# KV products and their fold into the output weights by single heads in small TensorE tiles, and another layout of the modulation weights at the start, in a transformer block on one Trainium2 core

## The chip, the cores and the metric

The kernel runs on one core of one Trainium2 chip. The time is device microseconds (us) of that core; lower is better. Every timed run below is of the fast state; a run taken once has no state, and it is used for its trace. Within the fast state runs still differ in the TensorE clock that was granted to them, by 0.1 to 0.5% of the span; that turns out to matter here. "PE" is TensorE (matmuls), "PEld" its weight loads, "DVE" VectorE, "ACT" ScalarE, "POOL" GpSimd, "SP" the engine that issues most DMA. A line number such as L98 is that of the kernel's source; nearly all matmuls go through one helper (L98), so they are told apart by the tiles that they write and read.

## The reference, cut to what matters

```python
x = A_x                                       # 1 x 2048 x 1024, bf16
mod = (silu(c) @ w_mod).reshape(1, 6, 1, -1)  # w_mod 1024 x 6144
sa, ca, ga, sb, cb, gb = ...                  # the six rows of mod
h = layernorm(x) * (1 + ca) + sa
x = x + ga * A(h)                             # linear attention, 32 heads of width 32
h = layernorm(x) * (1 + cb) + sb
x = x + gb * B(h)                             # SwiGLU, 1024 -> 3584 -> 1024

# A, for each head:
pq, pk = phi(q), phi(k)                       # phi(t) = t+1 if t > 0 else exp(t), + 1e-6
kv = einsum('bhsd,bhse->bhde', pk, v)         # 32 x 32 per head
z  = sum of pk over the sequence              # 32 per head
o  = (pq @ kv) / (pq @ z + 1e-6)
return concat_heads(o) @ wo
```

Two things matter. The matrix `kv` of a head is only 32 x 32, so a 128 x 128 product of four heads computes sixteen blocks and needs four. And nothing can start before `silu(c) @ w_mod` has given `sa` and `ca`.

## The kernel before

The sequence is cut into four parts of 512 rows. Each part gets its k and v; `kv` is summed over the parts; then `kv` is multiplied into `wo` once ("the fold", 16 matmuls), so that attention is one product of `pq` with the folded `wo`. The feed-forward part, some 600 us, follows and is not touched.

The KV products, four heads to a 128-wide matmul, with a 129th column of ones for `z`:

```python
def kv_phase(sc):
    for hg0 in range(0, HG, 3):
        nh = min(3, HG - hg0)
        kvp = acc_b("kvp")                    # acc_b: a PSUM bank, four in rotation
        kvv = kvp[:, 0:3 * (P + 1)].rearrange("p (g e) -> p g e", e=P + 1)
        for i in range(nh):
            for t in range(STC):
                mm(kvv[:, i, :], lhsT=pks[sc][:, t, (hg0 + i) * P:(hg0 + i + 1) * P],
                   rhs=vs[sc][:, t, hg0 + i, 0:P + 1], start=(t == 0), stop=(t == STC - 1))
        ...                                   # DVE adds it to kv_acc
```

The fold, after the 128 x 128 blocks have been masked to their diagonal 32 x 32 blocks (KVZ) and transposed (KVT):

```python
wf = [(hg, nb) for hg in range(HG) for nb in range(NNB)]
for qc in range(5, 11):
    q_phase(1 + qc // 8, qc % 8, qc % 8 + 1)            # 8 matmuls of 216 ns
    for hg, nb in wf[3 * (qc - 5):3 * (qc - 4)]:
        ps = acc_b("wf")
        w = wo[hg // 4][:, hg % 4, nb * NB:(nb + 1) * NB]
        mm(ps[:], lhsT=KVT[:, hg, :], rhs=w, start=True, stop=True)
        nc.scalar.copy(out=w, in_=ps[:])
```

The start. `c` comes as 8 values to a partition, and `w_mod` accordingly 8 consecutive rows to a partition; 20 matmuls on zeros (`keep_warm`) fill the time until the first x has been normalised:

```python
wm_v = w_mod.rearrange("(p j) n -> p j n", j=DC)
c_v = c.rearrange("o (p j) -> p (o j)", j=DC)
...
keep_warm(spare, 20)
with in_order(nc.vector, nc.scalar, nc.gpsimd):         # these engines keep program order
    nc.scalar.activation(out=scT[:], in_=c_sb[:], func=ACT.Silu)
    xns = [ln1_norm(*ln1_stats(0, t)) for t in range(3)]    # the last step is on ACT
    mod_ps = acc_b("mod_ps")
    pe_transpose_tile(hT, xns[0], 0, DC)
    keep_warm(spare, 1)
    mod_block(0, 1, 0, 4)                               # 32 matmuls of one column
    pe_transpose_tile(hT, xns[1], 1, DC)
    ...
    mod_block(0, 0, 0, 2)                               # needs the second w_mod block
    for cc in (0, 1):
        modulate(hT, cc, ca1T, saT, 0, H)
    mod_block(0, 0, 2, 4)
    ...
    k_mms(0, gs, accs, 0, 3)                            # "the first k matmuls"
```

Of the kernel before, what the change touches and what calls it, by code (L numbers as in the profile page):

```python
# [21 lines left out]
def kernel(  # L22
# [13 lines left out]
    nc = tc.nc  # L36
# [16 lines left out]
    FPB = FBW // P  # L53
    VW = P + 2
    GPT = 8
# [5 lines left out]
    wqkv_v = A_wqkv.rearrange("(c p) n -> p c n", p=P)  # L61
    wo_v = A_wo.rearrange("(c p) n -> p c n", p=P)
    wg_v = B_w_gate.rearrange("(c p) f -> p c f", p=P)
    wu_v = B_w_up.rearrange("(c p) f -> p c f", p=P)
    wd_v = B_w_down.rearrange("(f p) n -> p f n", p=P)
    wm_v = w_mod.rearrange("(p j) n -> p j n", j=DC)
    c_v = c.rearrange("o (p j) -> p (o j)", j=DC)

# [34 lines left out]
    def big(name, shape):  # L103
        return k8.tile([P] + shape, BF16, name=name, tag="k8")
# [8 lines left out]

    c_sb = const.tile([P, DC], BF16, name="c_sb")

# [62 lines left out]
    gb_bc = const.tile([P, D], BF16, name="gb_bc")  # L178
    kvs = k8.tile([P, HG * VW + HG * P], F32, name="kvs", tag="k8")
    kv_acc = kvs[:, 0:HG * VW].rearrange("p (g e) -> p g e", e=VW)  # L180
    kvb = kvs[:, HG * VW:].bitcast(BF16).rearrange("p (k g e) -> p k g e", k=2, e=P)
    KVZ, KVT = kvb[:, 0], kvb[:, 1]
    Zden = const.tile([P, HG, DH], BF16, name="Zden")
    kvmask = const.tile([P, P], BF16, name="kvmask")
    zmask = const.tile([P, HG, DH], BF16, name="zmask")
    sel = const.tile([P, HPC, P], BF16, name="sel")

    def build_masks():
        nc.gpsimd.memset(kvmask[:], 0.0)
        nc.gpsimd.memset(zmask[:], 0.0)  # L190
        for h in range(HPC):
            rs = slice(h * DH, (h + 1) * DH)
            nc.gpsimd.memset(kvmask[rs, rs], 1.0)
            for hg in range(HG):
                nc.gpsimd.memset(zmask[rs, hg, HG * h + hg:HG * h + hg + 1], 1.0)
            nc.gpsimd.memset(sel[h * DH:h * DH + 1, h, :], 1.0)
# [103 lines left out]
    def v_phase(sc):  # L300
        v = big("v", [STC, HG, VW])
        vs[sc] = v
        nc.gpsimd.memset(v[:, :, :, P:VW], 1.0)
        for t in range(STC):
            for nb in range(NNB):
                acc = acc_a()
                for cc in range(DC):
                    mm(acc[:], lhsT=hTs[sc][:, cc, t * P:(t + 1) * P],
                                     rhs=wv[cc // 4][:, cc % 4, nb * NB:(nb + 1) * NB],
                                     start=(cc == 0), stop=(cc == DC - 1))  # L310
                nc.scalar.copy(out=v[:, t, nb * 4:(nb + 1) * 4, 0:P], in_=acc[:].rearrange("p (g e) -> p g e", e=P))  # L311

    def q_phase(sc, lo=0, hi=DC):
        if lo == 0:
            pqs[sc] = big("pq", [HG, SCW])
        for qc in range(lo, hi):
# [4 lines left out]
            phi_to(pqs[sc][:, qc, :], acc[:])  # L321

    def kv_phase(sc):
        for hg0 in range(0, HG, 3):
            nh = min(3, HG - hg0)
            kvp = acc_b("kvp")
            kvv = kvp[:, 0:3 * (P + 1)].rearrange("p (g e) -> p g e", e=P + 1)
            for i in range(nh):
                for t in range(STC):
                    mm(kvv[:, i, :], lhsT=pks[sc][:, t, (hg0 + i) * P:(hg0 + i + 1) * P],  # L330
                                     rhs=vs[sc][:, t, hg0 + i, 0:P + 1], start=(t == 0), stop=(t == STC - 1))
            dst = kv_acc[:, hg0:hg0 + nh, 0:P + 1]
            if sc == 0:
                nc.vector.tensor_copy(out=dst, in_=kvv[:, 0:nh, :])
            else:
                nc.vector.tensor_tensor(out=dst, in0=dst, in1=kvv[:, 0:nh, :], op=ALU.add)

# [87 lines left out]
    with in_order(nc.vector, nc.scalar, nc.gpsimd):  # L425
        nc.scalar.activation(out=scT[:], in_=c_sb[:], func=ACT.Silu)
        xns = [ln1_norm(*ln1_stats(0, t)) for t in range(3)]
        mod_ps = acc_b("mod_ps")
        pe_transpose_tile(hT, xns[0], 0, DC)
        keep_warm(spare, 1)  # L430
        mod_block(0, 1, 0, 4)
        pe_transpose_tile(hT, xns[1], 1, DC)
        keep_warm(spare, 1)
        pe_transpose_tile(hT, xns[2], 2, DC // 2)
        keep_warm(spare, 3)
        mod_block(0, 0, 0, 2)
        for cc in (0, 1):
            modulate(hT, cc, ca1T, saT, 0, H)
        mod_block(0, 0, 2, 4)
        for cc in (2, 3):  # L440
            modulate(hT, cc, ca1T, saT, 0, H)
        k_mms(0, gs, accs, 0, 3)
# [6 lines left out]
        gs7, accs7 = k_groups[6:7], [acc_b("acc")]  # L449
        k_mms(0, gs7, accs7, 0, 4)  # L450
        mod_block(1, 0, 0, 2)
        for cc in (4, 5):
            modulate(hT, cc, ca1T, saT)
        k_mms(0, gs + gs7, accs + accs7, 4, 5)
        k_mms(0, gs[0:4], accs[0:4], 5, 6)
# [15 lines left out]
    for sc in range(NSC):  # L471
        if sc > 0:
            k_phase(sc, 0, 2)
            kv_phase(sc - 1)
            if sc >= 2:
                row = mod_rows(blks)
            k_phase(sc, 2, 4)
            if sc == 2:
                mod_bc(row)
            if sc == 3:  # L480
                mod_cols(row)
            k_phase(sc, 4, 8)
            if sc == 1:
                blks = mod_load([2 * D, 2 * D + NB, 5 * D, 5 * D + NB])
            if sc == 2:
                blks = mod_load([3 * D, 3 * D + NB, 4 * D, 4 * D + NB])
# [14 lines left out]
        if sc == 2:  # L501
            wo = load_w(wo_v, 0, "wo")
            for cc in range(DC):
                w = wo[cc // 4][:, cc % 4, :]
                nc.vector.tensor_tensor(out=w, in0=w, in1=ga_bc, op=ALU.mult)

    q_phase(1, 0, 2)
    kv_phase(NSC - 1)
    for h in range(2):
        hs = slice(4 * h, 4 * h + 4)  # L510
        nc.vector.tensor_tensor(out=KVZ[:, hs, :], in0=kv_acc[:, hs, 0:P],
                                in1=kvmask[:].unsqueeze(1).to_broadcast([P, 4, P]), op=ALU.mult)
        nc.vector.tensor_tensor(out=Zden[:, hs, :], in0=kv_acc[:, hs, P:P + 1].to_broadcast([P, 4, DH]),
                                in1=zmask[:, hs, :], op=ALU.mult)
    q_phase(1, 2, 4)
    tpk = acc_b("tp", (HG, P), BF16)
    for hg in range(HG):
        transpose(tpk[:, hg, :], KVZ[:, hg, :])
    nc.scalar.copy(out=KVT[:, 0:4, :], in_=tpk[:, 0:4, :])
    nc.vector.tensor_copy(out=KVT[:, 4:8, :], in_=tpk[:, 4:8, :])  # L520
    den_sum(0)
    den_spread(0)
    q_phase(1, 4, 5)
    wf = [(hg, nb) for hg in range(HG) for nb in range(NNB)]
    for qc in range(5, 11):
        q_phase(1 + qc // 8, qc % 8, qc % 8 + 1)
        for hg, nb in wf[3 * (qc - 5):3 * (qc - 4)]:
            ps = acc_b("wf")
            w = wo[hg // 4][:, hg % 4, nb * NB:(nb + 1) * NB]
            mm(ps[:], lhsT=KVT[:, hg, :], rhs=w, start=True, stop=True)  # L530
            nc.scalar.copy(out=w, in_=ps[:])

# [151 lines left out]
```

## Time and profile before

| | before |
|---|---|
| median of the first 4 runs | 844.27 us (843.91 to 845.21) |
| span of the profiled run | 841.5 us |
| PE busy | 833.8 us, 99% of the span |
| start of one matmul to the next in the stream, 512 / 128 / 129 / 1 columns (N) | 216 / 56 / 57 / 25 ns |
| one phase of KV products, four of them | 1.81 us |
| the fold, 16 matmuls | 3.46 us |

From the page of the kernel before, the busy time of each engine (us, share of the span, number of instructions), and the chain of work that ended last, by engine:

```profile
PE 833.8 (99%) x4289; PEld 385.5 (46%) x4289; DVE 306.8 (36%) x599; ACT 176.2 (21%) x268; POOL 55.6 (7%) x163
...
PE 98%; DMA 1%; SPq 0%; DVE 0%; issue 0%
```

The chain is PE nearly from end to end: what shortens PE's stream shortens the kernel, and what runs beside it does not. The chain in order of time (start, length in us, what) gives the parts that the change touches:

```profile
63.10 1.81 PE kvp L98 x32
...
161.85 0.45 PE tp L101 x8
...
166.42 0.65 PE wf L98 x3
167.06 1.73 PE acc L98 x8
168.79 0.65 PE wf L98 x3
```

A phase of KV products (`kvp`) is 32 matmuls at the 57 ns rate; the fold (`wf`) is five groups of three and one of one, each behind a q block of 1.73 us.

The start of the kernel before, from its timeline (start, length, engine, line, operation, out<-in, and in brackets how long the engine had been idle and what ended that):

```profile
1.21 7.00 PE L98 MATMUL acc<-sel 128*128 128x512 bf16 x20 [1.21 <-DVE sel L412]
...
5.23 0.21 ACT L426 ACTIVATE scT<-c_sb 128x8 bf16<-128x8 bf16 x1 [3.23 <-DMA c_sb<-in_c_dram]
...
10.69 0.95 PE L98 MATMUL mod_ps<-scT,wme 128*128 128x1 bf16 x32 [1.83 <-DMA wme<-in_w_mod_dram]
...
13.55 0.55 PE L98 MATMUL mod_ps<-scT,wme 128*128 128x1 bf16 x16
...
14.78 4.06 PE L98 MATMUL acc<-wk,hT 128*128 128x512 bf16 x18
```

Here Silu (`scT`) runs as soon as `c` has landed, PE waits for both `w_mod` blocks, and the first k matmul begins at 14.78 us.

### The profile page before, as it was taken

Reading aid. Unit: us, or ns where it says so; the run is one execution under the profiler, and the core shown is the slowest. Engines: PE = TensorE matmul, PEld = TensorE weight load, DVE = VectorE, ACT = ScalarE, POOL = GpSimd, SP = SyncE. Lnnn points to the kernel's source line nnn. Section 1 sums busy time; section 2 is a strip of 40 time slices with the busy share of each in tenths; the row PEclk is TensorE's granted clock in tenths of the full one; section 3 lists DMA queues with packets and bytes.
Section 4 is the critical chain, followed back from the end, with each engine's and each line's share of the span. In section 5 each row is a group of like instructions: output and inputs, shape, how many; then the busy total and the mean of one; then the engine's idle time right before and its main releaser. Section 6 shows DMA issues by size and latency. Waiting matters only on the chain.

```text
span 841.5 us, 10528 instructions
## 1 busy us (share of the span) xinstructions
PE 833.8 (99%) x4289; PEld 385.5 (46%) x4289; DVE 306.8 (36%) x599; ACT 176.2 (21%) x268; POOL 55.6 (7%) x163
## 2 busy tenths in 40 slices
PE   8999999999999999999999999999999999999998
PEld 4444444544444444444444444444444444444444
DVE  5656563467523324432221344211124432111122
ACT  3355353354211111101111010111110101111000
POOL 3011010112050001100000010000001100000000
PEclk9999999999999999999999999999999999999999
DMA  9895770029998545528434073581504629720011
GB/s 304 308 248 122 232 188 1 2 52 250 348 236 251 193 145 175 154 70 257 151 100 150 25 233 106 178 260 52 198 1 131 182 69 315 238 66 1 17 60 50
DMA packets 127232, 128.74 MB, mean 153 GB/s; under 512 B 33616, under 2 KB 108880, under 8 KB 126672
## 3 DMA queue, kind: packets, MB, share of 16 engines
q1 hardware_dynamic: 123600, 115.36, 45.7%
q0 software_dynamic: 3584, 12.72, 4.9%
q8 instruction: 33, 0.54, 0.3%
q14 instruction: 15, 0.12, 0.1%
HBM read 108.01 MB, written 12.71 MB: 143 GB/s over the span
## 4 chain that ended last, share of the span: by engine, by line
PE 98%; DMA 1%; SPq 0%; DVE 0%; issue 0%
PE acc L98 89%; PE a_ps L98 7%; DMA wme<-in_w_mod_dram 1%; PE kvp L98 1%; PE modr L98 0%; PE wf L98 0%; PE mod_ps L98 0%; PE den L98 0%; SPq L120 0%; PE tp L101 0%; PE bcr L98 0%; SPq L131 0%; SPq L125 0%; DVE hT L221 0%; PE mcol L98 0%
## 5 line engine op out<-in xcount | busy, mean ns | idle before, releaser
L98 PE MATMUL acc<-h2T,wgu 128*128 128x512 bf16 x1792 | 387.6, 379 | 0.0
L98 PEld LDWEIGHTS <-wgu 128*128 128x128 bf16 x1792 | 175.0, 98 | 211.6
L98 PE MATMUL acc<-wd,gu 128*128 128x512 bf16 (+2 forms) x924 | 196.1, 373 | 0.0
L591 DVE TENSOR_TENSOR gu<-acc,e 128x512 bf16<-128x512 f32 x112 | 77.5, 692 | 299.3 <-PE acc L98 296.5
L590 ACT ACTIVATE e<-acc 128x512 f32<-128x512 f32 x112 | 66.9, 597 | 374.8 <-PE acc L98 374.8
L98 PEld LDWEIGHTS <-gu 128*128 128x128 bf16 x924 | 89.2, 98 | 104.6
L98 PEld LDWEIGHTS <-hT 128*128 128x128 bf16 x512 | 49.4, 98 | 60.3 <-DVE hT L221 1.3
L612 DVE TENSOR_TENSOR e<-acc,gb_bc 128x512 f32<-128x512 f32 (+2 forms) x33 | 22.3, 676 | 131.3 <-PE acc L98 131.3
L98 PE MATMUL acc<-wk,hT 128*128 128x512 bf16 x256 | 57.6, 379 | 0.7 <-DVE hT L221 0.7
L98 PE MATMUL a_ps<-wo,pq 128*128 128x512 bf16 x256 | 57.4, 379 | 0.0
L98 PE MATMUL acc<-hT,wq 128*128 128x512 bf16 x256 | 57.1, 379 | 0.0
L98 PE MATMUL acc<-wv,hT 128*128 128x512 bf16 x256 | 55.9, 379 | 0.0
L273 ACT ACTIVATE eb<-acc 128x512 bf16<-128x512 f32 x64 | 37.9, 596 | 63.4 <-PE acc L98 60.3
L218 ACT ACTIVATE xn<-x,nmr,rstd 128x1024 bf16<-128x1024 f32 x16 | 19.8, 1240 | 126.3 <-POOL nmr L216 126.3
L274 DVE TENSOR_SCALAR eb<-eb 128x512 bf16<-128x512 bf16 x64 | 18.4, 291 | 58.7 <-ACT eb L273 58.6
L98 PEld LDWEIGHTS <-pq 128*128 128x128 bf16 x256 | 25.0, 98 | 30.3
L98 PEld LDWEIGHTS <-wq 128*128 128x128 bf16 x256 | 24.9, 98 | 29.8
L559 POOL DMA_DIRECT2D x_scratch<-x x16 | 9.6, 600 | 418.6 <-DVE x L552 418.6
L552 DVE TENSOR_TENSOR x<-a_ps,x_sb 128x512 f32<-128x512 f32 x32 | 22.1, 692 | 8.2 <-PE a_ps L98 8.1
L202 POOL TENSOR_TENSOR rstd<-veps,neg_half 128x1 f32<-128x1 f32 x32 | 18.0, 562 | 86.0 <-DVE veps L200 75.2
L311 ACT CAST v<-acc 128x512 bf16<-128x512 f32 x32 | 18.3, 582 | 22.0 <-PE acc L98 22.0
L615 DVE TENSOR_TENSOR ob<-e,x1r 128x512 bf16<-128x512 f32 (+2 forms) x33 | 22.3, 675 | 1.0
(72 smaller groups left out, 276.9 us busy)
## 6 DMA issues: line engine op xcount, KB each, us to landing
wgu<-in_B_w_gate_dram SPq DMA_DIRECT2D x28, 1024.0 KB, 7.5
wgu<-in_B_w_up_dram SPq DMA_DIRECT2D x28, 1024.0 KB, 8.7
x_sb<-in_A_x_dram SPq DMA_DIRECT2D x32, 256.0 KB, 6.7
wml<-in_w_mod_dram SPq DMA_DIRECT2D x8, 1024.0 KB, 8.6
x_scratch<-x POOLq DMA_DIRECT2D x16, 512.0 KB, 3.1
x1r<-x_scratch SPq DMA_DIRECT2D x31, 256.0 KB, 2.9
wd<-in_B_w_down_dram SPq DMA_DIRECT2D x7, 1024.0 KB, 5.6
rbc<-rden_scratch POOLq DMA_DIRECT2D x16, 256.0 KB, 5.2
```

What stands on the lines that cost most here:

```text
L98: return tc.keep_in_program_order(nc.tensor.matmul(out, lhsT=lhsT, rhs=rhs, start=start, stop=stop))
L202: nc.gpsimd.tensor_tensor(out=rstd[:, 0:n], in0=veps[:, 0:n], in1=neg_half[:].to_broadcast([P, n]), op=ALU.pow)
L218: nc.scalar.activation(out=dst, in_=src, func=ACT.Identity, bias=nmr[:], scale=rstd[:, 0:1])
L273: nc.scalar.activation(out=e[:], in_=acc, func=ACT.Exp)
L274: nc.vector.tensor_scalar(out=e[:], in0=e[:], scalar1=1.0, scalar2=PHI_EPS, op0=ALU.min, op1=ALU.add)
L311: nc.scalar.copy(out=v[:, t, nb * 4:(nb + 1) * 4, 0:P], in_=acc[:].rearrange("p (g e) -> p g e", e=P))
L552: nc.vector.tensor_tensor(out=x1[:, ns], in0=a_ps[:], in1=x_t[:, ns], op=ALU.add)
L559: nc.gpsimd.dma_start(out=x1_dram[st * P:(st + 1) * P, :], in_=x1[:])
L590: nc.scalar.activation(out=sg[:], in_=ps[0][:], func=ACT.Silu)
L591: gm = nc.vector.tensor_tensor(out=guT[sc][f // GPT][:, f % GPT, :], in0=ps[1][:], in1=sg[:], op=ALU.mult)
L612: nc.vector.tensor_tensor(out=yt, in0=y_ps, in1=gb_bc[:, ns], op=ALU.mult)
L615: nc.vector.tensor_tensor(out=ob, in0=yt, in1=x1r, op=ALU.add)
```

## The change

It does four things. The KV products go head by head: a matmul has 32 weight columns and writes 32 PSUM partitions, so that four heads stand side by side in the array ("column tiles"), and 64 moving columns (32 of v, 32 ones) in place of 129. The fold goes head by head too, in 32 x 32 tiles, 16 at once, which needs `wo` loaded in another order and 2 transposes in place of 8. `w_mod` rows are taken in blocks of 128, so that `c` can be loaded as 8 contiguous rows and turned by a matmul. And the first k matmuls and the modulation rows are re-paced.

The diff, cut to its core (masks, pool shapes and views are left out):

```diff
-    wm_v = w_mod.rearrange("(p j) n -> p j n", j=DC)
-    c_v = c.rearrange("o (p j) -> p (o j)", j=DC)
+    wm_v = w_mod.rearrange("(j p) n -> p j n", p=P)
+    c_v = c.rearrange("o (j p) -> (o j) p", p=P)
...
     def kv_phase(sc):
-        for hg0 in range(0, HG, 3):
-            ... (shown above)
+        kvp = acc_b("kvp", (HG, 2, DH))
+        for hg in range(HG):
+            for t in range(STC):
+                for i in range(HPC):
+                    mm(kvp[i * DH:(i + 1) * DH, hg, :, :],
+                       lhsT=pks[sc][:, t, hg * P + i * DH:hg * P + (i + 1) * DH],
+                       rhs=v_ones(vs[sc], t * D + hg * P + i * DH), start=(t == 0), stop=(t == STC - 1))
...
-        nc.scalar.activation(out=scT[:], in_=c_sb[:], func=ACT.Silu)
+        mod_ps = acc_b("mod_ps")
+        mm(mod_ps[:, 0:DC], lhsT=c_sb[:], rhs=ident[0:DC, 0:DC], start=True, stop=True)
+        nc.scalar.activation(out=scT[:], in_=mod_ps[:, 0:DC], func=ACT.Silu)
         xns = [ln1_norm(*ln1_stats(0, t)) for t in range(3)]
-        mod_ps = acc_b("mod_ps")
         pe_transpose_tile(hT, xns[0], 0, DC)
         keep_warm(spare, 1)
-        mod_block(0, 1, 0, 4)
         pe_transpose_tile(hT, xns[1], 1, DC)
         keep_warm(spare, 1)
+        mod_block(0, 1, 0, 4)
...
-        mod_block(0, 0, 0, 2)
-        for cc in (0, 1):
-            modulate(hT, cc, ca1T, saT, 0, H)
-        mod_block(0, 0, 2, 4)
-        for cc in (2, 3):
-            modulate(hT, cc, ca1T, saT, 0, H)
+        for lo, hi in ((0, 1), (1, 4)):
+            mod_block(0, 0, lo, hi)
+            for cc in range(lo, hi):
+                modulate(hT, cc, ca1T, saT, 0, H)
...
-        k_mms(0, gs7, accs7, 0, 4)
+        k_mms(0, gs7, accs7, 0, 2)
         mod_block(1, 0, 0, 2)
         for cc in (4, 5):
             modulate(hT, cc, ca1T, saT)
+        k_mms(0, gs7, accs7, 2, 4)
...
             kv_phase(sc - 1)
+            k_phase(sc, 2, 4)
             if sc >= 2:
                 row = mod_rows(blks)
-            k_phase(sc, 2, 4)
+            k_phase(sc, 4, 6)
...
-    q_phase(1, 4, 5)
-    (16 matmuls of 128 x 128 x 512, three behind each q block, shown above)
+    def fold_wo(h, nb):
+        ns = slice(nb * NB, (nb + 1) * NB)
+        ps = [acc_b("wf") for _ in range(4)]
+        for i in range(HPC):
+            for g in range(4):
+                rs = slice(g * DH, (g + 1) * DH)
+                mm(ps[g][i * DH:(i + 1) * DH, :], lhsT=KVT[rs, h, i * DH:(i + 1) * DH], rhs=wo[h][rs, i, ns],
+                   start=True, stop=True)
+        for g in range(4):
+            (nc.scalar.copy if g % 2 == 0 else nc.vector.tensor_copy)(out=wo[h][:, g, ns], in_=ps[g][:])
+
+    q_phase(1, 4, 6)
+    fold_wo(0, 0)
+    q_phase(1, 6, 8)
+    fold_wo(0, 1)
+    q_phase(2, 0, 2)
+    fold_wo(1, 0)
+    q_phase(2, 2, 3)
+    fold_wo(1, 1)
```

More of the change, by code (lines that the diff above doesn't have):

```diff
@@ L53 @@
     FPB = FBW // P
-    VW = P + 2
+    VT = STC * D
     GPT = 8
@@ L61 @@
     wqkv_v = A_wqkv.rearrange("(c p) n -> p c n", p=P)
-    wo_v = A_wo.rearrange("(c p) n -> p c n", p=P)
+    wo_v = A_wo.rearrange("(h g i e) n -> h g e i n", h=2, g=4, i=HPC)
     wg_v = B_w_gate.rearrange("(c p) f -> p c f", p=P)
@@ L112 @@
     x1_dram = dram.tile([S, D], F32, name="x1_scratch")
-    c_sb = const.tile([P, DC], BF16, name="c_sb")
+    c_sb = const.tile([DC, P], BF16, name="c_sb")
     x_tiles = {}
@@ L178 @@
     gb_bc = const.tile([P, D], BF16, name="gb_bc")
-    kvs = k8.tile([P, HG * VW + HG * P], F32, name="kvs", tag="k8")
-    kv_acc = kvs[:, 0:HG * VW].rearrange("p (g e) -> p g e", e=VW)
-    kvb = kvs[:, HG * VW:].bitcast(BF16).rearrange("p (k g e) -> p k g e", k=2, e=P)
-    KVZ, KVT = kvb[:, 0], kvb[:, 1]
+    kvs = k8.tile([P, HG * (2 * DH + 1)], F32, name="kvs", tag="k8")
+    kv_acc = kvs[:, 0:HG * (DH + 1)].rearrange("p (g e) -> p g e", e=DH + 1)
+    kvb = kvs[:, HG * (DH + 1):].bitcast(BF16)
+    KVB = kvb[:, 0:HG * DH].rearrange("p (g e) -> p g e", e=DH)
+    KVT = kvb[:, HG * DH:].rearrange("p (h e) -> p h e", e=P)
     Zden = const.tile([P, HG, DH], BF16, name="Zden")
-    kvmask = const.tile([P, P], BF16, name="kvmask")
     zmask = const.tile([P, HG, DH], BF16, name="zmask")
@@ L188, in build_masks @@
     def build_masks():
-        nc.gpsimd.memset(kvmask[:], 0.0)
         nc.gpsimd.memset(zmask[:], 0.0)
@@ L192, in build_masks @@
             rs = slice(h * DH, (h + 1) * DH)
-            nc.gpsimd.memset(kvmask[rs, rs], 1.0)
             for hg in range(HG):
@@ L300, in v_phase @@
     def v_phase(sc):
-        v = big("v", [STC, HG, VW])
+        v = big("v", [VT + DH])
         vs[sc] = v
-        nc.gpsimd.memset(v[:, :, :, P:VW], 1.0)
+        nc.gpsimd.memset(v[:, VT:], 1.0)
         for t in range(STC):
@@ L310, in v_phase @@
                                      start=(cc == 0), stop=(cc == DC - 1))
-                nc.scalar.copy(out=v[:, t, nb * 4:(nb + 1) * 4, 0:P], in_=acc[:].rearrange("p (g e) -> p g e", e=P))
+                nc.scalar.copy(out=v[:, t * D + nb * NB:t * D + (nb + 1) * NB], in_=acc[:])
     def q_phase(sc, lo=0, hi=DC):
@@ L321, in q_phase, with v_ones @@
             phi_to(pqs[sc][:, qc, :], acc[:])
+    def v_ones(v, lo):
+        head = v[:, lo:lo + DH]
+        return bass.AP(head.tensor, head.offset, [list(head.ap[0]), [VT - lo, 2], [1, DH]])
     def kv_phase(sc):
-        for hg0 in range(0, HG, 3):
-            nh = min(3, HG - hg0)
-            kvp = acc_b("kvp")
-            kvv = kvp[:, 0:3 * (P + 1)].rearrange("p (g e) -> p g e", e=P + 1)
-            for i in range(nh):
-                for t in range(STC):
-                    mm(kvv[:, i, :], lhsT=pks[sc][:, t, (hg0 + i) * P:(hg0 + i + 1) * P],
-                                     rhs=vs[sc][:, t, hg0 + i, 0:P + 1], start=(t == 0), stop=(t == STC - 1))
-            dst = kv_acc[:, hg0:hg0 + nh, 0:P + 1]
-            if sc == 0:
-                nc.vector.tensor_copy(out=dst, in_=kvv[:, 0:nh, :])
-            else:
-                nc.vector.tensor_tensor(out=dst, in0=dst, in1=kvv[:, 0:nh, :], op=ALU.add)
+        kvp = acc_b("kvp", (HG, 2, DH))
+        for hg in range(HG):
+            for t in range(STC):
+                for i in range(HPC):
+                    mm(kvp[i * DH:(i + 1) * DH, hg, :, :], lhsT=pks[sc][:, t, hg * P + i * DH:hg * P + (i + 1) * DH],
+                       rhs=v_ones(vs[sc], t * D + hg * P + i * DH), start=(t == 0), stop=(t == STC - 1))
+        kvv = kvp[:].rearrange("p g k e -> p g (k e)")[:, :, 0:DH + 1]
+        if sc == 0:
+            nc.vector.tensor_copy(out=kv_acc, in_=kvv)
+        else:
+            nc.vector.tensor_tensor(out=kv_acc, in0=kv_acc, in1=kvv, op=ALU.add)
     def mod_load(cols):
@@ L481 @@
                 mod_cols(row)
-            k_phase(sc, 4, 8)
+            k_phase(sc, 6, 8)
             if sc == 1:
@@ L501 @@
         if sc == 2:
-            wo = load_w(wo_v, 0, "wo")
+            wo = [big("wo", [4, D]) for _ in range(2)]
+            for h in range(2):
+                for g in range(4):
+                    nc.sync.dma_start(out=wo[h][g * DH:(g + 1) * DH, :, :], in_=wo_v[h, g])
             for cc in range(DC):
@@ L508 @@
     kv_phase(NSC - 1)
-    for h in range(2):
-        hs = slice(4 * h, 4 * h + 4)
-        nc.vector.tensor_tensor(out=KVZ[:, hs, :], in0=kv_acc[:, hs, 0:P],
-                                in1=kvmask[:].unsqueeze(1).to_broadcast([P, 4, P]), op=ALU.mult)
-        nc.vector.tensor_tensor(out=Zden[:, hs, :], in0=kv_acc[:, hs, P:P + 1].to_broadcast([P, 4, DH]),
-                                in1=zmask[:, hs, :], op=ALU.mult)
-    q_phase(1, 2, 4)
-    tpk = acc_b("tp", (HG, P), BF16)
-    for hg in range(HG):
-        transpose(tpk[:, hg, :], KVZ[:, hg, :])
-    nc.scalar.copy(out=KVT[:, 0:4, :], in_=tpk[:, 0:4, :])
-    nc.vector.tensor_copy(out=KVT[:, 4:8, :], in_=tpk[:, 4:8, :])
+    nc.vector.tensor_copy(out=KVB, in_=kv_acc[:, :, 0:DH])
+    nc.vector.tensor_tensor(out=Zden[:], in0=kv_acc[:, :, DH:DH + 1].to_broadcast([P, HG, DH]),
+                            in1=zmask[:], op=ALU.mult)
+    q_phase(1, 2, 4)
+    tpk = acc_b("tp", (2, P), BF16)
+    for h in range(2):
+        transpose(tpk[:, h, :], KVB[:, 4 * h:4 * h + 4, :].rearrange("p g e -> p (g e)"))
+    nc.vector.tensor_copy(out=KVT, in_=tpk[:])
     den_sum(0)
     den_spread(0)
-    q_phase(1, 4, 5)
-    wf = [(hg, nb) for hg in range(HG) for nb in range(NNB)]
-    for qc in range(5, 11):
-        q_phase(1 + qc // 8, qc % 8, qc % 8 + 1)
-        for hg, nb in wf[3 * (qc - 5):3 * (qc - 4)]:
-            ps = acc_b("wf")
-            w = wo[hg // 4][:, hg % 4, nb * NB:(nb + 1) * NB]
-            mm(ps[:], lhsT=KVT[:, hg, :], rhs=w, start=True, stop=True)
-            nc.scalar.copy(out=w, in_=ps[:])
+    def fold_wo(h, nb):
[6 more added lines that the diff above has]
+                   start=True, stop=True)
+        for g in range(4):
+            (nc.scalar.copy if g % 2 == 0 else nc.vector.tensor_copy)(out=wo[h][:, g, ns], in_=ps[g][:])
[7 more added lines that the diff above has]
+    fold_wo(1, 1)
     h2Ts = {}
```

## The prediction

> **What bounds the kernel.** TensorE. The page shows PE busy 833.8 of 841.5 us; the chain of waits is PE for 98%. Matmul start times in the trace give the cost in the stream: 216 ns at N=512, 55.8 at N=128/129, 25 at N=1. Gaps above that stand only in the first 27 us: 1.8 us before 10.69 (first w_mod block), 0.3 before 13.55 (second), 0.2 before 14.78, 0.13 at 18.8, 0.65 at 23.46 (hT modulation on DVE), 0.2 at 26.9. Only fewer PE nanoseconds or smaller early gaps can save time.
>
> **Costs.**
>
> 1. KV products. Before: 4 phases of 32 matmuls 128x129, 1.81 us each (chain of waits), no mode switch. After: 128 matmuls 32x64 a phase in four column tiles side by side. The den matmuls (128*32, N=128) show four starting within 11 ns and the next four 56 ns after: four cost one. At N=64 I estimate 29 ns per four, 0.94 us a phase. Entering and leaving this form costs some 95 ns each (modr to acc 311 against 216 ns; tp to den 149 against 56); the Trainium skill, "TensorEngine Tiling (Array Packing)", Tiling Modes, says that changing the mode drains TensorE, and these gaps agree. So 1.13 us a phase at best, saving 2.7 in all. No run here shows eight instructions per 29 ns, and small weight loads may limit it; I count 2.2 us.
> 2. Fold of KV into wo. Before: 16 x 216 ns = 3.46 us. After: four groups of 16 matmuls 32x32, N=512, meant to run at once; estimate 216 + 15 starts x 4 + 2 x 95 = 0.47 us a group, 1.9 in all. The skill, "TensorE: Matmul & The Clock Gate", Part 3, gives 10.6x for 16 such tiles; here the switches eat much of it. Saves 1.5 us. Half the copies go to DVE; the last group comes only one q block (1.73 us) after the one before and may wait some tenths for PSUM.
> 3. Transposes 8 to 2: 6 x 56 ns = 0.33 us.
> 4. Start. c lands as 8 rows, not 128 pieces of 16 bytes: 0.2 us of DMA. But Silu now waits for a matmul behind the 20 warm-up matmuls, about 8.04 us instead of 5.23, and stands first on ACT: xn starts near 8.5 instead of 6.23. The chain xn, transposes, copies then ends about when the second w_mod block lands (13.5), so little shows, and an earlier landing would help little. One chunk instead of two before the first k matmuls: 0.2 us. Two k matmuls moved behind a mod block fill 0.43 us of the 0.65 us gap. I count 0.5 us net. Row blocks of 128 move the same 1 KB pieces; I expect no bandwidth change that matters.
> 5. The rest (wo in eight loads, v copies, masks, later mod rows) is off the path.
>
> Sum 4.5 us, nearly all on PE, the critical path.
>
> **Prediction.** 839.8 us, 8 in 10 within 837.4 to 842.8. Faster by over 2%: 0.01; within: 0.98; slower: 0.01.
>
> **What would show it.** Chain of waits: kvp pieces of 1.1 us, not 1.81; wf groups of 0.45 us; first k matmuls at 14.3-14.9 us; the gap at 23.46 down by 0.4; Silu near 8.3, not 5.2. Everything after 215 us keeps its length.
>
> **What would make it wrong.** Small matmuls run at an instruction or weight-load limit (kvp 1.8 us or more); the 16 tiles don't overlap; a PSUM wait at the last fold; the late Silu pushes the first k matmuls past 15 us; or the second w_mod block lands over 1 us earlier and the chain behind Silu is shorter than I think.

## The result, and the profile after

The changed kernel took 839.6 us (median of 4 runs, 838.95 to 840.95), the kernel before 844.27. The ratio of the fast runs is 0.9945, with a 95% interval of 0.9928 to 0.9962: faster beyond its noise. A ratio here is the mean time of one kernel's fast runs over that of the other's fast runs of the same rounds, so it is not quite the ratio of the medians. The prediction was 839.8.

The page of the changed kernel, the same two lines:

```profile
PE 829.5 (99%) x4716; PEld 380.5 (45%) x4716; DVE 307.7 (37%) x597; ACT 171.5 (20%) x259; POOL 54.8 (7%) x158
...
PE 97%; DMA 2%; DVE 0%; SPq 0%; issue 0%; ACT 0%
```

PE's busy time fell by 4.3 us though it has 427 matmuls more. The chain in order of time:

```profile
9.17 12.05 DMA wme<-in_w_mod_dram
...
62.15 1.15 PE kvp L98 x128
...
158.67 0.11 PE tp L101 x2
...
162.90 0.36 PE wf L98 x16
163.27 3.56 PE acc L98 x16
...
167.19 3.58 PE acc L98 x16
170.77 0.02 issue
170.79 0.61 ACT eb L271
...
171.75 0.69 DVE pq L274
172.44 1.21 DVE wo L533 x2
173.64 0.04 issue
173.69 0.43 PE wf L98 x13
```

The first line is a later `w_mod` block that lands at 21.22 us: in this trace the chain of the start runs over it, and not over the first k matmul; more on this below. The KV phases and the first three groups of the fold are as short as predicted. The fourth is not: the chain leaves PE and runs over two DVE copies of the third group (`DVE wo`) to the last 13 of the 16 matmuls. The start of the changed kernel, from its timeline:

```profile
1.21 5.89 PE L98 MATMUL acc<-sel 128*128 128x512 bf16 x20 [1.21 <-DVE sel L412]
...
7.25 0.18 ACT L428 ACTIVATE scT<-mod_ps 128x8 bf16<-128x8 f32 x1 [5.25 <-PE mod_ps L98]
7.32 3.50 ACT L216 ACTIVATE xn<-x_sb,nmr,rstd 128x1024 bf16<-128x1024 bf16 x3
...
12.32 0.34 PE L98 MATMUL mod_ps<-scT,wme 128*128 128x1 bf16 x8
...
13.63 4.05 PE L98 MATMUL acc<-wk,hT 128*128 128x512 bf16 x18
```

Silu now waits for PE and holds back the normalisation behind it, as predicted, and yet the first k matmul came 1.15 us earlier, not 0.2. The 20 warm-up matmuls took 5.89 us in this run and 7.00 in the one before: that differs from run to run, as the experiments show.

**Where the 4.7 us are.** Three marks divide a trace: the start of the first v matmul, the start of the first matmul of attention (`a_ps`), and the end of the span.

| stretch | before (3 traces) | changed (this trace and its repetition) |
|---|---|---|
| start to first v matmul | 31.86, 33.45, 31.88 us | 30.91, 32.14 us |
| first v to first `a_ps` | 151.66 us in all | 148.33 us in both |
| first `a_ps` to the last matmul | 654.25 us in all | 654.25 us in both |
| last matmul's start to the end | 3.70 to 3.71 us | 3.33 us in both |

So 3.33 us came in the middle and 0.38 us at the very end, the same in every pair of traces. What scatters from run to run lies in the start alone: span minus first v is 809.62 or 809.63 us in all three traces of before, 805.91 or 805.92 in both of the changed kernel.

The middle, from the start times of matmuls, counting what lies between the rates of the streams on either side:

| | before | changed | saved |
|---|---|---|---|
| four KV phases, with the switches around them and the modulation rows' | 7.45 | 5.17 | 2.27 us |
| fold | 3.45 | 2.64 | 0.81 us |
| KV transposes | 0.54 | 0.205 | 0.335 us |

These sum to 3.42. Some 0.08 us was given back behind the small tiles: the first full matmul after a group of them takes 226 or 227 ns to the next in place of 216, and there are eight such groups more than before. With the end it makes 3.71 us that no run takes away. The rest of the measured difference must lie in the start, and that is where the runs scatter.

### The profile page after: what moved, and what is told of

Same layout as the page of the kernel before. It is cut to its first block, busy times and chain, and to the rows that moved or that the text cites. A ratio compares the mean times of both kernels' runs of the same rounds, so it can differ in the third digit from the quotient of the medians.

```text
span 836.8 us, 11376 instructions
## 1 busy us (share of the span) xinstructions
PE 829.5 (99%) x4716; PEld 380.5 (45%) x4716; DVE 307.7 (37%) x597; ACT 171.5 (20%) x259; POOL 54.8 (7%) x158
## 4 chain that ended last, share of the span: by engine, by line
PE 97%; DMA 2%; DVE 0%; SPq 0%; issue 0%; ACT 0%
PE acc L98 88%; PE a_ps L98 7%; DMA wme<-in_w_mod_dram 2%; PE kvp L98 1%; PE modr L98 0%; PE den L98 0%; SPq L120 0%; DVE wo L533 0%; PE wf L98 0%; PE mod_ps L98 0%; PE bcr L98 0%; DVE pq L274 0%; ACT eb L271 0%; DVE hT L219 0%; PE mcol L98 0%
```

## The experiments

Twelve runs were made (the changed kernel once more, nine edits of it, the kernel before twice) in three groups, each group on one chip beside its own runs of the kernel before (medians 843.66, 844.56 and 844.40 us). The theories to test at first were these. (1) The last fold's wait is for PSUM, and goes if it is given time. (2) The small KV matmuls are limited by how fast instructions arrive, not by their columns. (3) Each change of the tile form has its own cost. (4) The start gained by the new layout; the rivals are that the re-pacing did it, or chance. A fifth came out of the runs: (5) the clock.

### The changed kernel again

No edit.

> The changed kernel unaltered, to time it beside its variants and to sample its start once more. Expected 839.2 to 840.2 us, ratio 0.9935 to 0.9955. Main theory of the start: the second w_mod block lands earlier (12.15 us against 13.5 in the one trace of each) because c no longer comes as 128 pieces of 16 bytes and the rows are read in blocks; then it lands by 12.6 again. Rival: which of the 16 DMA engines falls behind is chance; then it may land anywhere from 11.5 to 14.

It took 839.79 us (838.83 to 840.18), ratio 0.9952 (0.9939 to 0.9964). The second `w_mod` block landed at 13.18 us in place of 12.15, and the warm-up matmuls took longer:

```profile
1.21 7.38 PE L98 MATMUL acc<-sel 128*128 128x512 bf16 x20 [1.21 <-DVE sel L412]
...
8.74 0.18 ACT L428 ACTIVATE scT<-mod_ps 128x8 bf16<-128x8 f32 x1 [6.73 <-PE mod_ps L98]
...
15.12 4.04 PE L98 MATMUL acc<-wk,hT 128*128 128x512 bf16 x18
```

From Silu to the first k matmul it is 15.12 - 8.74 = 6.38 us here, and 13.63 - 7.25 = 6.38 us in the first trace. In all six traces in which Silu follows all 20 warm-up matmuls this interval is 6.38 or 6.39 us, while Silu itself lies anywhere from 7.25 to 8.74. So in the changed kernel the chain behind Silu sets the first k matmul, and not the landing of `w_mod`; my theory of the landing missed what binds. An earlier first k is not always an earlier first v, though. In eight of the twelve traces at full clock the first v comes 17.02 to 17.08 us after the first k; in the other four, whose first k came before 14.0 us (13.32 to 13.97), it is 17.28 to 17.91 us, and their chains run over a later `w_mod` block that landed at 20.1 to 21.2 us. Silu moves because 7 to 14 of the warm-up matmuls, by the run, start some 427 ns apart in place of 216. The Trainium skill, "TensorE: Matmul & The Clock Gate", Part 1, says that the array starts at half its clock, that the window which releases it runs free of the kernel's start, and that the number of slow matmuls of one kernel therefore varies (6, 11 or 14 in its example). This agrees, and shows what follows when something on the critical path is queued behind them.

### The layout undone, and the whole start undone

```diff
# layout undone: w_mod and c as before, Silu straight from c; the order of matmuls stays
-        mm(mod_ps[:, 0:DC], lhsT=c_sb[:], rhs=ident[0:DC, 0:DC], start=True, stop=True)
-        nc.scalar.activation(out=scT[:], in_=mod_ps[:, 0:DC], func=ACT.Silu)
+        nc.scalar.activation(out=scT[:], in_=c_sb[:], func=ACT.Silu)
# start undone: the same, and mod blocks and first k matmuls in the order of before
```

> The changed kernel with w_mod rows and c laid out as before and Silu straight from c; the new order of the first k matmuls stays. Main theory: the second w_mod block lands near 13.5 us as before, the first k matmuls begin near 14.6, and the time rises by about 0.5 to 0.9 us over the changed kernel's. Rival (chance, and the late blocks of the DMA stream bind, not the first): landing of the second block scattered as in the run beside it, and the time within 0.3 us of the changed kernel's.

> The changed kernel with the whole start as before (layout, c, Silu, order of mod blocks and first k matmuls). If the start is worth what the two traces show (0.95 us at the first v matmul), the first v matmul is again at 31.7 to 32.0 us and the time 0.9 us over the changed kernel's. If the re-pacing alone is the worth (my 0.43 us), it lies 0.4 to 0.5 us over the run with only the layout undone; if the layout alone, equal to it.

With the layout undone: 839.77 us (838.25 to 842.54), ratio 0.9960 (0.9943 to 0.9977). With the whole start undone: 838.88 us (838.66 to 840.09), ratio 0.9944 (0.9932 to 0.9956). Neither is told apart from the changed kernel (0.9952) by its time, and the ladder of differences that I expected isn't there: my theory of the start fell. The first v matmul came at 34.29 us in the one trace and at 31.57 in the other. From first v to `a_ps` both take 148.33 us like the changed kernel, so whatever the start does, it does before that mark. (The start-undone trace also lost 0.5 us to a `wd` load issued near 308 us that landed late, at 314.85 us, which no other trace shows.)

The 34.29 us are the clue. The run with the layout undone has a granted clock of 0.996 where the other has 1.000. Its trace, in stretches of 3 us (length, busy time of each engine, then the granted clock, DMA share and GB/s):

```profile
12.00:15.00 3.00, 1.83 (x37) 1.14 (x35) 0.96 (x3) 0.59 (x1) 0.00 (x0) 0.83 1.06 383
15.00:18.00 3.00, 3.00 (x9) 1.06 (x7) 2.67 (x8) 0.00 (x0) 0.09 (x1) 0.50 1.11 352
18.00:21.00 3.00, 3.00 (x9) 1.03 (x7) 0.72 (x1) 0.00 (x0) 2.81 (x39) 0.53 1.07 322
21.00:24.00 3.00, 3.00 (x41) 1.90 (x40) 1.02 (x4) 1.66 (x2) 0.00 (x0) 1.00 1.10 328
```

From 14.0 to 20.8 us, just when the first k matmuls run, TensorE had half its clock: a k matmul starts every 427 ns in place of 216 there, so 9 stand in 3 us. The DMA is as fast as ever. This is theory 5: in some runs the clock falls back in the start, and what the starts differ in is how often. It is followed up below.

### The fold spaced

```diff
-    q_phase(1, 4, 6)
+    q_phase(1, 4, 5)
     fold_wo(0, 0)
-    q_phase(1, 6, 8)
+    q_phase(1, 5, 7)
     fold_wo(0, 1)
-    q_phase(2, 0, 2)
+    q_phase(1, 7, 8)
+    q_phase(2, 0, 1)
     fold_wo(1, 0)
-    q_phase(2, 2, 3)
+    q_phase(2, 1, 3)
     fold_wo(1, 1)
```

> The changed kernel with the four folds moved so that two q blocks (3.45 us) stand before the last one as before the others. Theory: the last fold's 0.8 us stall is a wait for PSUM buffers that two DVE copies release; it goes, each fold takes 0.37 us to the next matmul, and the time falls by 0.7 to 0.8 us against the changed kernel's. Rival: the stall belongs to the fold itself (its operand wo is overwritten in place by the fold before), or the earlier first fold meets the reciprocal on DVE and waits in its turn; then a stall of 0.4 us or more remains at one of the folds.

It took 838.64 us (837.94 to 838.75), ratio 0.9939 (0.9927 to 0.9950), and the chain of its trace has no DVE at the fold:

```profile
161.78 0.36 PE wf L98 x16
162.15 3.56 PE acc L98 x16
...
169.63 0.36 PE wf L98 x16
170.00 3.56 PE acc L98 x16
173.55 0.36 PE wf L98 x16
173.92 5.29 PE acc L98 x24
```

From first v to `a_ps` it takes 147.52 us, 0.81 less than the changed kernel. The stall was the wait of the last group for PSUM banks which the third group's copies held, and those copies stood on DVE behind the q block's own work; given two q blocks, it is gone entirely. Spacing alone does not tell a wait for the banks from one for `wo`, which the same copies write; the changed kernel's trace does. There the first two matmuls of the last group start at once, at 172.88 us, and the next two at 173.09 and 173.69, each 0.05 us after one of the two DVE copies ended: they waited bank by bank. Theory 1 holds.

### The modulation rows straight behind the KV products

```diff
             kv_phase(sc - 1)
-            k_phase(sc, 2, 4)
             if sc >= 2:
                 row = mod_rows(blks)
-            k_phase(sc, 4, 6)
+            k_phase(sc, 2, 6)
```

> The changed kernel with the modulation rows put straight behind the KV products again, as in the kernel before; both use column tiles (128*32) now. Theory: each change of the tile form costs 93 to 100 ns, and between two groups of the same form there is none; the two pairs of changes go, 0.38 us in all, and the interval from kvp to modr has no gap above 60 ns. Rival: the gap belongs to the group (its first weights or PSUM), not to the form; then 95 ns stand between kvp and modr and the time stays within 0.1 us.

It took 839.06 us (838.15 to 839.44), ratio 0.9937 (0.9917 to 0.9956). PE's timeline of the changed kernel around these groups:

```profile
90.97 1.22 PE L98 MATMUL kvp<-v,pk 128*32 128x64 bf16 x128
92.12 3.63 PE L98 MATMUL acc<-wk,hT 128*128 128x512 bf16 x16
95.68 1.91 PE L98 MATMUL modr<-wml,sc 128*32 128x512 bf16 x32
```

and of this kernel:

```profile
91.86 1.22 PE L98 MATMUL kvp<-v,pk 128*32 128x64 bf16 x128
92.89 1.92 PE L98 MATMUL modr<-wml,sc 128*32 128x512 bf16 x32
```

From the first `kvp` matmul to the matmul behind it is 1.15 us where the form changes (92.12 - 90.97), and 1.03 us where it does not; the 93 ns on entering `modr` go as well. First v to `a_ps` takes 147.91 us, 0.42 less than the changed kernel, where I had estimated 0.38. Theory 3 holds: the cost is the change of form, 93 ns on the way in and some 100 to 120 on the way out, and it is not there between two groups of the same form. The Trainium skill, "TensorEngine Tiling (Array Packing)", Tiling Modes, says that changing the mode drains TensorE, and that changing only the tile does not; this run shows both halves.

### c earlier

```diff
-    keep_warm(spare, 20)
+    keep_warm(spare, 10)
...
         nc.scalar.activation(out=scT[:], in_=mod_ps[:, 0:DC], func=ACT.Silu)
+        keep_warm(spare, 10)
```

> The changed kernel with c's matmul after 10 of the 20 warm-up matmuls in place of after all 20. Silu then runs near 5.7 to 6.0 us in place of 7.25 and xn of the first tile near 6.2 in place of 7.43. Theory (the start is bound by the DMA stream, from the first k matmuls on by later blocks landing near 21.2 us): the first k matmuls gain at most 0.3 us, the first v matmul none, time within 0.2 us of the changed kernel's. Rival (the chain behind Silu binds): the first v matmul comes 0.5 us or more earlier.

It took 838.95 us (838.47 to 841.96), ratio 0.9945 (0.9924 to 0.9965): not told apart from the changed kernel. In its trace Silu ran at 6.59 us, because `c` had landed only just before (PE stood 1.30 us waiting for it; in the kernel before Silu ran at 5.23; that eight rows would land earlier than 128 pieces, as I had assumed, is not what this shows). The first k matmul came at 13.42 us and the first v at 30.44, the earliest of all traces, so for that trace the rival, the chain behind Silu, is right. One of its six timed runs, the slowest, has a clock of 0.996, the others 1.000.

### 32 columns in place of 64 in the KV products (wrong result)

```diff
-                    mm(kvp[i * DH:(i + 1) * DH, hg, :, :], ..., rhs=v_ones(vs[sc], t * D + hg * P + i * DH), ...)
+                    mm(kvp[i * DH:(i + 1) * DH, hg, 0, :], ..., rhs=vs[sc][:, (32 columns of v)], ...)
```

> Wrong result on purpose: the KV products read 32 columns in place of 64 (no ones, z set to 1), all else as in the changed kernel. Theory: after the first some 32 matmuls[...], TensorE gets one weight load and matmul in 8.3 ns whatever their size (in the changed kernel four take 29 ns at first and 33 ns later); a phase then still takes 0.95 to 1.1 us to the next matmul. Rival: the 33 ns are the 64 columns; then four take 16 to 20 ns and a phase 0.6 to 0.75 us.

One look, 839.23 us; the result is wrong, as intended. PE's timeline, first the changed kernel:

```profile
62.08 1.22 PE L98 MATMUL kvp<-v,pk 128*32 128x64 bf16 x128
63.23 1.04 PE L98 MATMUL acc<-wk,hT 128*128 128x512 bf16 x4
```

then this one:

```profile
62.73 1.20 PE L98 MATMUL kvp<-v,pk 128*32 128x32 bf16 x128
63.86 1.47 PE L98 MATMUL acc<-wk,hT 128*128 128x512 bf16 x5
```

Half the columns save 26 ns of 1154 (1128 from the first `kvp` matmul to the matmul behind). The start times tell why. The first 32 matmuls take 243 ns with 64 columns and 217 ns with 32; four start within 10 ns or so and the next four come 29 and 25 ns after them. From about the 32nd on, the matmuls come one by one, on average every 8.2 ns in the one and 8.4 in the other: the size no longer matters. So after a first burst TensorE runs at the rate at which it gets weight loads and matmuls, 8.3 ns a pair, or 33 ns for four. A rival is that the weight loads, equal in both runs, take that long themselves; but in the burst of this run they, too, start four in 25 ns. Theory 2 holds as far as the columns go; which step on the way to TensorE sets the 8.3 ns, no run tells. That the burst is what the queue had stored is an inference: the skill, "TensorE: Matmul & The Clock Gate", in its table of the engine, gives the queue a depth of 64, and 32 matmuls with their 32 weight loads are 64 instructions.

### Both orders at once

The edits of the spaced fold and of the modulation rows, together.

> The changed kernel with both orders that the other runs try: folds spaced by two q blocks, modulation rows behind the KV products. If both effects are real and independent, 0.8 + 0.38 us below the changed kernel's, some 838.4 us, ratio to the kernel before near 0.993. If one of them gives back later, less than 0.8 us.

It took 838.21 us (837.39 to 838.84), ratio 0.9929 (0.9911 to 0.9947). First v to `a_ps` takes 147.10 us: 1.23 less than the changed kernel, just the sum of 0.81 and 0.42. This is the fastest median.

### All three, with the new and with the old layout

The edits of the last kernel and the earlier `c`; the second run has `w_mod` and `c` in the layout of before instead.

> The changed kernel with all three: folds spaced, modulation rows behind the KV products, c's matmul after 10 of the 20 warm-up matmuls. In seven traces with the new layout the first k matmul came 6.38 us after Silu wherever Silu followed all 20 warm-up matmuls, and Silu came at 7.25 to 8.74 us as 7 to 14 of them ran at the slow clock; with c early it was bound by the second w_mod block instead (13.42 us). Theory: first k at 12.8 to 13.6, first v at 29.9 to 30.7 us, and from first v to a_ps 147.1 us; some 837 to 837.8 us, ratio near 0.992. Rival: later blocks of the DMA stream then bind and first v stays at 31 us or later.

> The same as the run before it, but w_mod rows and c laid out as in the kernel before (Silu straight from c, so early as well). In three traces with the old layout the second w_mod block landed at 12.6 to 13.6 us, in seven with the new one at 11.4 to 13.2. Theory: the layout makes blocks land about 1 us earlier; this run is then 0.5 to 2 us slower than its neighbour and first v comes at 31.3 us or later. Rival (chance): both within 0.4 us.

With the new layout: 839.29 us (837.61 to 839.71), ratio 0.9933 (0.9918 to 0.9948). With the old one: 839.83 us (837.65 to 840.83), ratio 0.9943 (0.9926 to 0.9959). The first v matmul came at 30.80 and at 31.59 us. The intervals overlap, so the times don't separate the layouts, and the earlier `c` did not beat the kernel without it (0.9929). Four of the five timed runs of the first and four of the six of the second had a clock of 0.998 or less; the one run of the first at full clock took 837.61 us, its other four 838.40 to 839.71. So part of what the earlier `c` may have gained was lost to the clock; one run at full clock is too few to say how much. In the trace of the first, PE also stood 0.47 us for a later `w_mod` block, at 21.16 us.

### The kernel before, twice more

No edit.

> The kernel before once more, for its trace: where its start and its end lie. If its one trace was typical, the second w_mod block lands near 13.5 us, first k at 14.5 to 15, first v at 31.6 to 32.2, and the end 3.7 us after the last matmul begins (3.33 in all traces of the changed kernel). If the start scatters, first v lies over 32.5 or under 31.5.

> As the run before it: a third trace of the kernel before. From first v to a_ps it must take 151.66 us in both if nothing but the start scatters.

The spans were 843.1 and 841.5 us. First v lay at 33.45 and 31.88 us; the rest is the same to 0.01 us, the end included. The granted clock was 0.996 in the first and 1.000 in the second. The stretches of the first, columns as above:

```profile
12.00:15.00 3.00, 2.70 (x37) 1.31 (x36) 1.68 (x7) 0.53 (x1) 0.00 (x0) 0.50 1.06 378
15.00:18.00 3.00, 2.78 (x7) 1.03 (x7) 2.26 (x7) 0.00 (x0) 0.94 (x4) 0.50 1.13 336
18.00:21.00 3.00, 3.00 (x19) 1.52 (x18) 0.34 (x1) 0.00 (x0) 2.49 (x42) 0.87 1.12 332
```

and of the second:

```profile
12.00:15.00 3.00, 2.12 (x38) 1.41 (x38) 2.01 (x8) 0.10 (x1) 0.00 (x0) 1.00 1.06 397
```

With all traces at hand, the last of the second `w_mod` block's sixteen completions came at 12.63 to 13.57 us in the six traces with the old layout (mean 13.12) and at 11.39 to 13.18 us in the eight with the new one (mean 12.23). So the new layout probably does land earlier by some 0.9 us, of which 0.3 us is already there when the block is issued (2.97 to 2.99 us against 3.29 to 3.30); that is a comparison over several chips and few traces, and whether the order of the rows or the missing 128 small pieces of `c` did it, no run tells. It shows little in the time because Silu, moved behind the warm-up, takes the earlier landing away again.

### The clock in all timed runs

In both traces with a clock of 0.996 the half clock lasted 6.83 us, beginning at 12.0 and at 14.0 us; half of 6.83 us is 0.4% of the span, which is the 0.004 that is missing. (0.998 would fit 3.4 us; no trace has such a run.) The 33 timed runs of the kernel before fall apart accordingly: 14 runs with a clock of 0.999 or 1.000 took 841.99 to 843.75 us (mean 842.99), 19 with 0.998 or less 844.01 to 847.12 (mean 845.07). Of the changed kernel and its variants with the same start (first comparison, repetition, spaced fold, modulation rows, both) 1 timed run of 26 was at 0.998 or less.

With the runs at full clock alone, against those of the kernel before on the same chip (mean of them 843.03, 842.76, 843.31 us):

| kernel | full-clock runs | mean | below the kernel before |
|---|---|---|---|
| changed, again | 5 of 5 | 839.59 | 3.44 us |
| layout undone | 3 of 6 | 838.96 | 4.07 us |
| start undone | 6 of 6 | 839.15 | 3.88 us |
| fold spaced | 5 of 5 | 838.50 | 4.53 us |
| modulation rows next | 6 of 6 | 838.91 | 3.85 us |
| c early | 5 of 6 | 839.00 | 3.76 us |
| spaced and rows next | 6 of 6 | 838.17 | 4.59 us |
| all three, new layout | 1 of 5 | 837.61 | 5.70 us |
| all three, old layout | 2 of 6 | 838.02 | 5.29 us |

At full clock the changed kernel is 3.44 us faster, which is the 3.71 us of the middle and the end, less 0.3. By the scatter of these runs each figure of the table is good to some 0.3 or 0.4 us (standard error, more where one to three runs are behind it), so the 0.3 is not told from nothing; but the three other kernels with the same start, less what their traces gain in the middle, give 3.72, 3.43 and 3.36 us, so the 0.5 us expected of the start is not there. Both starts with an early Silu (layout undone, start undone) lie ahead of it, by no more than twice their noise. On average over all runs of that chip the kernel before takes 843.90 us, 0.87 more than at full clock, and the changed kernel 839.59; 3.44 + 0.87 = 4.31 us is the whole difference. So the part of the gain that the middle and the end don't explain, some 0.6 us here, comes from runs in which the kernel before fell back to half its clock and the changed one did not.

Why it falls back is only inferred. The Trainium skill, "TensorE: Matmul & The Clock Gate", Part 1, says that an idle window of some 3.4 us brings the half clock back, and that the window runs free. The half clock here lasted two times 3.41 us, which agrees; but in the trace that fell back at 12.0 us PE's longest gap before it was 1.4 us (8.4 to 9.8), followed by one-column matmuls and transposes. The kept traces allow one look at how little work is enough. Cut on each trace's own changes of the clock into windows of 3.41 us, they hold 91 such windows at full clock that begin between the end of the warm-up and 27 us. The two after which the clock fell streamed the fewest columns through PE of all, 2,600 and 2,637, where some 8,100 would fit at 216 ns for 512; the next have 2,756 and more. Transposes are counted in this; without them a window of 1,044 columns kept its clock while one of 1,576 lost it. Two falls are a lead and no proof. The kernel before waits there for the first `w_mod` block with one warm-up matmul; the changed kernel spreads transposes and warm-up matmuls over that time. Not explained by this is the run with the start undone: it has the start of before and none of its six runs fell back, where half of the kernel before's runs on that chip did (5 of 11). That stays open.

### The end

When the last output has been sent, SP waits for every semaphore in a fixed order, two to an instruction, some 62 ns each. From the trace of the kernel before, then of the changed one (us before the end, semaphores; cut):

```
before                          changed
-2.37  118, 116                 -2.00  118, 116
-1.33  101, 115                 -1.93  101, 115
-1.26  103, 114                 -1.87  103, 114
-1.20  104, 113                 ...
...                             -1.63  107, 100
-0.96  109, 102                 -0.96  109, 102
-0.90  110, 107                 -0.90  110, 108
```

The last output's DMA counts on semaphore 101 in the kernel before and on 109 in the changed one, as DMAs take semaphores in rotation and the number of DMAs differs. In the kernel before the landing ends the third wait of the list and the remaining ones follow it; in the changed kernel those were done while the DMA was under way. Six instructions of 62 ns are 0.37 us, and the span after the last landing is 1.34 us against 0.97. The waits of SP's queue in the last microseconds, as the profile lists them (total us, times, longest), of the kernel before:

```profile
SPq L679 <- DMA out_dram<-ob: 1.0, 1, 1.0
```

and of the changed kernel:

```profile
SPq L690 <- DMA out_dram<-ob: 0.6, 1, 0.6
```

No run moved this on purpose; that the position in the list makes the difference is read from the traces (three of one kind, eleven of the other, each always the same).

## Why the prediction was right

The total was right, 839.6 against 839.8 us, but not for every reason given. The terms, as the prediction had them and as the traces show them:

| term | predicted | measured |
|---|---|---|
| KV products | 2.2 us | 2.27 us |
| fold | 1.5 us | 0.81 us |
| transposes | 0.33 us | 0.335 us |
| start at full clock | 0.5 us | -0.3 us (not told from 0) |
| half clock in the start | not thought of | 0.87 us on average (second comparison) |
| end | 0 | 0.38 us |

- **KV products: right, for the reason given.** 1.15 us in the chain of waits against "1.1 us, not 1.81". The best case (29 ns for four, 2.7 us) was cut to 2.2 because no run showed instructions arriving that fast. They don't: 33 ns for four once the first burst is over.
- **Switches: right.** 93 ns in and 100 to 120 out, against "some 95 ns each".
- **Fold: the mechanism was right, the last group's wait was mis-sized.** A group costs 0.37 us to the next matmul and 0.09 on entry, 0.46 against "0.47 us a group". The step that failed is "may wait some tenths for PSUM", which the sum then left out: the wait was 0.80 us, half of the whole expected gain. It could have been worked out beforehand: the q block's Exp, its two DVE steps and the fold's two copies stand in a row before the last bank comes free (0.61 + 0.30 + 0.69 + 1.21 = 2.8 us in the chain), and one q block gives only 1.73 us.
- **Start: the chain was right, its size open.** "Silu near 8.3" is the middle of the 7.25 to 8.74 seen; "first k matmuls at 14.3 to 14.9" holds for three of the six traces with that start (14.49, 14.54, 14.75), while 13.63, 14.98 and 15.12 lie outside. "An earlier landing would help little" is what the constant 6.38 us from Silu to first k shows. Failed: "0.2 us of DMA" from `c`, which lands no earlier; probably "no bandwidth change that matters" from the row blocks; and "I count 0.5 us net": at full clock the start gained nothing that shows. The re-pacing, counted at 0.2 + 0.43 us, brought under 0.1. "One chunk instead of two" changed nothing: from the landing of the second block to the first k it is 1.27 us in the trace of before and 1.25 in the two traces with the new order where that landing sets it (the earlier `c`; all three with the old layout). And the gap on DVE `hT` did fall from 0.71 to 0.25 us, but a wait of 0.35 us for `xn` now stands before the last transposes, so that the first v follows the first k by 17.02 us (repetition) against 17.08. Silu's delay cost about what the earlier landing brought: by an estimate from the six traces with that start, their first k lies on average 1.1 us behind the landing of the second block plus 1.25 us, and that landing came some 0.9 us earlier.
- **The clock: missed.** The page of before shows a granted clock of 1.0 and I took that for every run; more than half of the timed runs (19 of 33) had less, and their loss of some 2 us was already in the median that I started from.
- **The end: missed.** "Everything after 215 us keeps its length" holds to 0.01 us for PE and failed for the last 0.38 us, which come from the order of the closing waits. It made up for half of the fold's shortfall, by luck.

So the errors, -0.7 us in the fold and -0.8 at the start, +0.4 at the end and +0.9 for the clock, nearly cancelled, which is luck: the timed difference was 4.67 us by the medians of the first comparison and 3.87 us by those of the second, against 4.5 predicted. A single total that fits is no proof of its terms.

## What to carry to other kernels

In this kernel small-tile matmuls save PE time up to a limit of about 8.3 ns for each weight load with its matmul, and each change of the tile form costs some 0.2 us in and out; put groups of the same form next to each other, and give the copies that empty their PSUM banks as much time as the slowest engine's queue needs before the next group. Keep whatever the critical path needs out of the queue behind warm-up matmuls, whose duration varies from run to run (the trace that did so had the earliest first v, though its time was not told apart). When the difference is under 1%, sort the timed runs by granted clock and compare stretches between marks in the traces rather than whole times: here the start carried nearly all of the noise, and the other stretches repeated to some 0.02 us, but for one late load of 0.5 us in one trace.

## What the Trainium skill lacked or had wrong

- "TensorE: Matmul & The Clock Gate", Part 1 ("start-to-start never drops below ≈25 ns however small N is"): true here within one column tile (25 ns for 32 columns). What the page lacks is the sustained rate of small tiles: after the first 32 or so, one weight load with its matmul every 8.3 ns, whether it has 32 or 64 columns.
- "TensorEngine Tiling (Array Packing)", Tiling Modes: the drain on a change of mode has no figure. Here 93 ns on entering and 100 to 120 ns on leaving, and none between two groups of the same mode.
- "TensorE: Matmul & The Clock Gate", Part 3 (10.6x for 16 tiles of 32 x 32, N=512): inside a stream of full matmuls the 16 took 0.46 us with both switches, against 16 x 216 ns = 3.46 us for as many full matmuls, so 7.5x.
- "TensorE: Matmul & The Clock Gate", Part 1, calls the warm-up ramp under 1% of a typical kernel's span and advises not to fit to it. That is so here (7 to 14 slow matmuls of 20), yet it moved Silu, and with it the first k matmul, by 1.5 us between runs, more than several of the effects studied.
- The same Part says that one idle window of 3.4 us brings the half clock back, and its rule is to have no PE gaps over about that; of many short gaps it tells one case, without a figure. What it lacks is how much work in a window is too little. Here the half clock came back for 6.83 us with no gap over 1.4 us before it, after windows of 2,600 and 2,637 columns; a granted clock of 0.998 or less was seen in 19 of 33 timed runs of one kernel.
- No page that I read has the closing waits: SP goes through the semaphores in a fixed order at some 62 ns for each instruction, and where the last DMA's semaphore stands in that order was worth 0.37 us.
